# Linear attention and a soft mixture of experts on one core: three more expert weight tiles held during attention, by giving two of their slots, two input buffers and the accumulator a second use

## The chip, the cores and the metric

The kernel runs on one core of a Trainium2 chip. The metric is the device time of one execution in microseconds (us), less is better. On the core, TensorE (PE) multiplies matrices, VectorE (DVE), ScalarE (ACT) and GpSimd (POOL) do the elementwise work, and SyncE (SP) issues every DMA; each engine runs its own instructions in program order and waits on semaphores for the others.

## The reference, cut to what matters

```python
def _attn_ref(q, k, v, w_phi):            # 8 batches, 8 heads, 576 tokens, 64 columns
    def phi(x):
        proj = np.einsum('bhsd,df->bhsf', x, w_phi)
        proj = proj - np.max(np.abs(proj), axis=-1, keepdims=True)
        return np.concatenate([np.exp(proj), np.exp(-proj)], axis=-1)
    q_p, k_p = (phi(q), phi(k))
    kv = np.einsum('bhsf,bhsd->bhfd', k_p, v)
    z = np.sum(k_p, axis=2)
    num = np.einsum('bhsf,bhfd->bhsd', q_p, kv)
    den = np.einsum('bhsf,bhf->bhs', q_p, z)[..., None] + 1e-06
    return (num / den)

def _moe_ref(x, phi, w1, w2):             # x [4608, 512], 8 experts with 4 slots each, 1024 hidden
    logits = x @ phi
    d = softmax of logits over the tokens
    slot_input = d.T @ x
    slot_out[e] = max(slot_input[e] @ w1[e], 0) @ w2[e]
    c = softmax of logits over the slots
    return c @ slot_out
```

## The kernel before, in words

Heads are worked off in 32 units `u` (a pair of batches, one head, 1152 tokens, 9 tiles of 128). The keys and queries of all units lie end to end and are cut into 72 blocks `b` of 512 tokens. `proj(b)` multiplies a block of keys and the block of queries two back with `w_phi` into PSUM (`psk`, `psq`). `kmax` and `kfac` make the keys' scale factors `mk`, `kneg_exp` and `kpos_exp` the features `kf`, `vals` (POOL, L317) scales the values `vt` into `vs`, `kvmm` and `kvmid` sum `kvp` over the tokens; `num` multiplies the queries' features with it (`psn`), `scale` and `comb` join the two halves in `un`, and `denom`, `recip` and `divide` (POOL) write the attention's output into `xc` and `xn`.

These outputs are taken up in nine groups of 512 tokens. A group is turned on PE (`turn` or, for the last three, `fturn`), copied to SBUF tiles `xT`, multiplied with `moe_phi` (`logits`), and enters the running softmax over tokens (`gmax` to `update`, the accumulator is `acc`). The softmax over slots is worked on later in `call`. Then follow the experts: `layer1` (tiles `hp`, L905), `layer2` (`yp`, L979) and the outputs (`pso`, L999; copied to `o`, written to `out`).

The experts' weights are 64 tiles `wt` of 512 KB. As many as fit are loaded while attention runs (`weight`, 30 slots). Further slots lie over the buffers of attention and open when these close (`close`, `opened`), and the rest reuse the slots of the first layer's weights. `room` works the number of slots out from the sizes. Input tiles `xs` (512 KB, two blocks) have three buffers, values `vt` two.

All DMAs go through SP's one queue in program order. `load` adds two waits to it: `behind` (not before PE has passed a mark) and `deep` (not before the DMA two places earlier has landed, while attention runs).

```python
        deep = 4 if len(sent) < 9 else 2 if len(wpools) < 4 else 4 if len(wpools) < 10 else 6
```

The order of attention's work on every engine is the string `ORDER`, a letter for each step; it was made by a planner that is not part of the program. `TAIL` sets the order of layer 2 and the outputs in the same way.

Of the kernel before, what the change touches and what calls it, by code (L numbers as in the profile page):

```python
# [43 lines left out]
TRI = 3  # L44
BUFS = {'xs': 3, 'kf': 3, 'vs': 2, 'vt': 2, 'qf': 3, 'un': 2, 'xT': 4, 'xc': 2}
PICK = {'xcopy': 'adda', 'kvcopy': 'daad', 'zde': 'a'}
TOP = 212900


def room(bufs):  # L50

    parts = [XW * 4, XW * 4, XW * 4 + 2560, 4096, 4096, 4096 + bufs["vs"] * 2080 + bufs["vt"] * 2368,
             2 * 4096, 4096 + 2 * 1056, bufs["un"] * 2368, bufs["xT"] * 2048, (bufs["xc"] + 1) * G * DM * 4]
    return [int(n) // 4096 for n in np.cumsum([TOP - sum(parts)] + parts)]


class Plan:
# [42 lines left out]
ORDER = (  # L100
    "bbccbfaafhhldckiddkicgjdnoggfkglcnomhljjqbdgbdemmaprnpjjstovrrvfhfiihimmwwknvwfckndbyjjllocgehimpjqgdgfhmmprmflo"
    "jscldeihiqajmrptvwmkjbrzApnAAvvwawfsmogmejaychidpknfcgldzuhcdtlforgAjAgimknvpwrrvwohirfhjbbvwqsmykkicdnnzcgjoeml"
    "ofpjAAhitmrplrlkfqvnwvwvwjdomkmepngAcAscjtddfmolalrahryzigmfjjAvxxhkpAqrrwvvmmhknnwwyziisooceclpAAAAddgjknobgfhm"
    "tvlqrwrrjfivvwhjbwimpmmgcknstvwlknjaaocdgelxdmfyzAppAhoqrvwrvwicbbsycgrjtkdlnrffzAhodivrhibvAkwmwggnocvwfAAllhkk"
    "jjcieanyzmmoAldnojjpBpfCBhVVmmiqCbxcepddsADErftrvwgjgAmvawmhrxxFGknlopivjwmfhiBCBjHmVIcgCqdcllkjjs:eVnfDhoKqgpmr"
    "irEFkdgmLtnoJvvpxjrfhismmkHvnwcyzIwAwydzabol:tcejpfbhcKAiddaxllfhigrknAomrgAAAvwGLqvprrjmwgvxbksnowknojctefclhdm"
    "gprlfhjmxviyqdwvpfjjmmazArkwvAihnAgjjciwsepoykndctrrlxfhidlmmrovwvbggkpzfqvwjmmwkclcAJhjlAAiyempMaansfhnmptofozr"
    "hdAgvrbvirkwwbcvnrdijoAwmjmdqkggykAstneplclffocljnmoxxjhqviwdrpknozmhigdgrrvrAAAstvjaxkrfwwnjjvohwckyiNnckvwvwzA"
    "cemdAdloyzfAAnhimmpplodfBBghiVqsrVjfbbmrCCtvgjlrvAhAeapiwDvMEkOanoFmmpBGwwyVHCBVjIcgkjbd:fcchlrilCmmddgjxxnoqkPf"
    "DnoKehiExggsLmpjtrjmvvfFhblqmwprkwvnwizmaHIscjybAAepcddJ:allotfhGicKfhiAzgrmdvqwpsrxknojrrvALgAAxknkfovwwthlimNv"  # L110
    "cdycjgjllMenfgzxoprhikmmdgqvrjpjwnvoafmmwwyhcdjlAcdksAAgjfhiieznpgbmmrfbhpiarlqtvjrkoNvvwwwrAAmmysknepcAbndkjjfc"
    "zglltmvoOAhnixooAAfrmvpdrvrqwknomjmwgwhicayszdeptkvwbcfhlilgcljmApfrdjmaqnoksAAndgogvhitbrvrknrrwwycvwvwfhfhxzjj"
    "AAvwicylzxknlooemmAAppBBOdiqVgbkCVnosjcdgCfhdjPixrrmatmAlvrwvwAfvDEkhjjnwbgcFemodpmfhJHpialqBBijIgx:VmsmexCpkVCn"
    "JccoddgDtfrjbEllmhFjMgvwfrGmrknpvjwmqmhjiivHwI:aKNPxKsLkncyzoxGLfhcllyzermddAAatppqAgjrrgstokkvwnvnoAAAvmorifhcw"
    "wkvbwdcdfijexhiggncdjmplofhajyrvlmrbfmjmJgjpjhiizkAcAAwclqkvwnoyepmmddgnsgfprtlhiorMflqrvvjzhmmxivrwwAaewkyAscnt"
    "zknplfAdckbnlgoorrvoQvwAvqAhmwwjdiknrjjfmoyzmhismAAgcpepNllRSQqAtvQQARSknRrSjmvwOsTRRRwktpQQRSOryzSSyzSnrAAovwrr"
    "QUvwyyzzTAXvvRRMYwUwyzZAXRyzNSAAXXQQ4Y0Z0SS2oOTWW3W7YYZ68Q02295533665+58+5P58798+8+Q//=P<!!P=!!")

# [7 lines left out]
def tile_kernel(ctx: ExitStack, tc, xT, vv, w, phi, w1, w2, cst, out):  # L126
# [13 lines left out]
    stacks = {k: ExitStack() for k in ("x1", "x2", "x0", "k0", "k1", "v", "q1", "q2", "u", "t", "c")}  # L140

    def numbered(i, shape, name):
        return pall.tile(shape, F32, tag=f"b{i}", name=name)
# [12 lines left out]
    qp[0:2] = [pool("q1", "q1", bufs=1, side="right")] * 2  # L156
    vp = pool("v", "vp", bufs=1, side="right")
    kp = [pool(f"k{i}", f"k{i}", bufs=1, side="right") for i in (1, 0)][::-1] + [vp]
    xp = [pool(f"x{i}", f"x{i}", bufs=1, side="right") for i in (0, 2, 1)]
    xp = [xp[0], xp[2], xp[1]]  # L160

    def xtile(e):
        return xp[e % 3].tile([128, XW], F32, tag="xs", name="xs")
# [23 lines left out]
    def load(t, x, behind=False):  # L187
        i = nc.sync.dma_start(t, x).ins
        if behind and seen[2]:
            tc.add_manual_dep(i, seen[2], mybir.DependencyInfo(mybir.DependencyClass.Sync, mybir.DependencyReason.DATA), reason="behind")  # L190
        deep = 4 if len(sent) < 9 else 2 if len(wpools) < 4 else 4 if len(wpools) < 10 else 6
        if len(sent) > 3:
            tc.add_manual_dep(i, sent[-deep].name, mybir.DependencyInfo(mybir.DependencyClass.Sync, mybir.DependencyReason.DATA), reason="deep")
        sent.append(i)
# [10 lines left out]
        load(vt[u], vv[u // H, u % H], u > 1)  # L205


    call = const.tile([128, NTT, NS], F32, name="call")
    xs[1] = xtile(1)
    wx = xp[0].tile([128, 512 + FE], F32, name="wx")  # L210
    wd = wx[:, 512:512 + FE]
    load(wx, w)
    for i in 0, 512:
        load(xs[1][:, i:i + 512], xT[0][:, i:i + 512])
# [497 lines left out]
    for s in *range(NK - 4), NK - 3, NK - 2, NK - 4, NK - 1:  # L712
# [48 lines left out]
        for i, group in enumerate(groups if final else ()):  # L761
            key, pair = (m, i), (m, i // 2)

            def turn(key, group, n=n, got=got):
                ps = got[key] = bank(("turn", key), [128, 4, 128], "psx")
                for o, (kc, j) in enumerate(group):
                    nc.tensor.transpose(ps[:, o], tile4(n, j)[:, kc * 128:(kc + 1) * 128], ident)  # L767

            def keepit(key, pair, group, d, got=got, xTs=xTs):
                if (pair, "t") not in got:  # L770
                    got[pair, "t"] = xTtile(pair)
                t = got[pair, "t"][:, key[1] % 2]
# [149 lines left out]
    with tc.manual_schedule(engines={SP, PE, ACT, DVE, POOL}):  # L922
# [143 lines left out]
```

## Time and profile before

| | |
|---|---|
| median of 3 runs | 313.62 us (312.73 to 315.37) |
| the profiled execution | 316.0 us, span 314.2 us |
| PE busy | 297.1 us, 95% of the span |
| first block's products / experts' first product / last output product | 3.65 / 260.28 / 302.55 us after the span's start |

The profile is of one execution. A time in the trace is counted from the start of the span; 1.8 us of the profiled execution lie outside the span.

### The profile page before, as it was taken

How to read it: one execution, taken by the hardware profiler on the slowest of the kernel's cores; microseconds unless marked ns; L12 is line 12 of the kernel's file. 1: busy time of each engine (PE TensorE's matmuls, PEld its weight loads, DVE VectorE, ACT ScalarE, POOL GpSimd, SP SyncE). 2: the span in 40 equal slices, each digit the busy share in tenths (PEclk: the TensorE clock that was granted, in tenths of full speed). 3: DMA queues.
4: the chain of work that ended last, by engine and by line, in shares of the span. 5: the costliest groups of instructions: out<-in, count | busy, mean ns of one | idle time of the engine just before them, and what ended most of it. 6: DMA issues, size and time to landing. Idle time of an engine off the chain costs nothing.

```text
span 314.2 us, 17960 instructions
## 1 busy us (share of the span) xinstructions
PE 297.1 (95%) x7736; PEld 255.7 (81%) x7736; DVE 237.5 (76%) x706; ACT 229.4 (73%) x696; POOL 149.8 (48%) x309
## 2 busy tenths in 40 slices
PE   7999999999999799999989999999999999999970
PEld 4999999989889799998889999979998853386730
DVE  2878888968997598888968999888898867324560
ACT  4999998988878788889888889888998361003450
POOL 1657757555275566546557576446675400200000
PEclk9999999999999999999999999999999999999996
DMA  7625457667466757367666776775447999999896
GB/s 245 198 93 173 137 157 232 188 215 204 162 198 236 219 185 231 90 209 218 218 218 192 225 202 221 215 231 167 159 139 256 353 360 398 409 406 364 323 394 271
DMA packets 23119, 73.13 MB, mean 233 GB/s; under 512 B 2560, under 2 KB 2816, under 8 KB 23040
## 3 DMA queue, kind: packets, MB, share of 16 engines
q1 hardware_dynamic: 23040, 71.99, 68.5%
q8 instruction: 61, 1.00, 1.3%
q14 instruction: 18, 0.15, 0.2%
HBM read 62.54 MB, written 9.44 MB: 229 GB/s over the span
## 4 chain that ended last, share of the span: by engine, by line
PE 86%; DMA 4%; DVE 2%; ACT 2%; issue 2%; SPq 1%; POOL 0%; DVEq 0%; ACTq 0%
PE kvp L182 23%; PE psn L182 21%; PE psk L182 14%; PE psq L182 6%; PE hp L905 4%; PE yp L979 4%; PE psl L182 3%; PE psx L185 2%; DMA out<-o 2%; PE pso L999 2%; PE pss L182 2%; DMA xs<-xT 2%; PE psx L767 1%; PE psh L957 1%; DVE o L1003 1%
## 5 line engine op out<-in xcount | busy, mean ns | idle before, releaser
L317 POOL TENSOR_TENSOR vs<-vt,mk 128x520 f32<-128x520 f32 (+3 forms) x96 | 79.5, 838 | 42.7 <-DMA vt<-vv 13.4
L182 PE MATMUL kvp<-vs,kf 128*64 128x65 f32 (+1 forms) x2560 | 89.3, 223 | 2.9 <-POOL vs L317 1.8
L182 PEld LDWEIGHTS kvp<-vs,kf 128*64 128x64 f32 (+1 forms) x2560 | 82.8, 137 | 9.1 <-issue 4.8
L182 PE MATMUL psn<-kvs,qf 128*64 128x65 f32 x2304 | 78.7, 223 | 2.2 <-issue 2.1
L182 PEld LDWEIGHTS psn<-kvs,qf 128*64 128x64 f32 x2304 | 72.5, 138 | 6.7 <-issue 5.0
L182 PE MATMUL psq<-xs,wx 64*64 64x512 f32 x288 | 70.5, 601 | 1.3 <-DMA xs<-xT 0.8
L182 PE MATMUL psk<-wx,xs 64*64 64x128 f32 x1120 | 69.4, 272 | 0.0
L362 DVE TRANSPOSE_TENSOR_REDUCE mts<-psq 128x16 f32<-128x512 f32 x72 | 49.4, 701 | 13.0 <-PE psk L182 10.5
L182 PEld LDWEIGHTS psk<-wx,xs 64*64 64x64 f32 x1120 | 58.4, 133 | 0.0
L304 DVE TENSOR_REDUCE mk<-psk 128x4 f32<-128x512 f32 x72 | 47.9, 674 | 10.6 <-PE psk L182 9.6
L322 ACT ACTIVATE kf<-psk 128x512 f32<-128x512 f32 x72 | 43.0, 599 | 11.8 <-PE psk L182 8.1
L367 ACT ACTIVATE qf<-psq 128x512 f32<-128x512 f32 x72 | 42.4, 590 | 5.7 <-PE psk L182 3.2
L446 POOL TENSOR_TENSOR xc<-un,dn 128x256 f32<-128x256 f32 x62 | 37.8, 614 | 17.1 <-DVE dn L431 11.5
L325 ACT ACTIVATE kf<-psk 128x512 f32<-128x512 f32 x72 | 42.9, 600 | 0.0
L370 ACT ACTIVATE qf<-psq 128x512 f32<-128x512 f32 x72 | 42.1, 592 | 0.1
L411 DVE TENSOR_TENSOR un<-psn,eq 128x195 f32<-128x195 f32 x96 | 32.4, 345 | 7.6 <-PE psn L182 4.0
L416 DVE TENSOR_TENSOR un<-psn,un 128x195 f32<-128x195 f32 x96 | 32.0, 353 | 1.3
L378 ACT ACTIVATE mh<-mts 32x36 f32<-32x36 f32 x128 | 29.5, 230 | 3.9 <-DVE mts L362 1.6
L384 DVE TENSOR_REDUCE eq<-mh 32x9 f32<-32x36 f32 x128 | 26.1, 204 | 2.6 <-ACT mh L378 1.2
L1003 DVE COPY o<-pso 128x384 f32<-128x384 f32 x24 | 12.1, 551 | 10.3 <-PE pso L999 10.2
L182 PEld LDWEIGHTS psq<-xs,wx 64*64 64x64 f32 x288 | 15.6, 132 | 4.6 <-DMA xs<-xT 1.1
L307 ACT ACTIVATE mk<-mk 128x4 f32<-128x4 f32 x72 | 14.8, 208 | 4.5 <-DVE mk L304 3.9
(128 smaller groups left out, 307.7 us busy)
## 6 DMA issues: line engine op xcount, KB each, us to landing
wt<-w SPq DMA_DIRECT2D x64, 512.0 KB, 5.5
xs<-xT SPq DMA_DIRECT2D x35, 512.0 KB, 4.3
vt<-vv SPq DMA_DIRECT2D x32, 292.5 KB, 3.5
out<-o SPq DMA_DIRECT2D x24, 384.0 KB, 4.9
xs<-xT SPq DMA_DIRECT2D x2, 256.0 KB, 4.5
wx<-w SPq DMA_DIRECT2D x1, 320.0 KB, 2.9
cs<-cst SPq DMA_DIRECT2D x1, 128.0 KB, 2.4
phs<-phi SPq DMA_DIRECT2D x1, 64.0 KB, 3.8
```

What stands on the lines that cost most here:

```text
L182: counted(nc.tensor.matmul(*a, **k).ins, 4)
L304: nc.vector.tensor_reduce(km[b][:, 2], kx[b], axis=AX, op=ALU.max, apply_absolute_value=True)
L317: nc.gpsimd.tensor_tensor(vs[b][:, :, g + t0:g + t1], v[:, t0:t1].unsqueeze(1).broadcast_to([128, 2, n, 65]), km[b][:, 0:2, g + t0:g + t1] ...
L322: nc.scalar.activation(kf[b][:, 1], kx[b], AF.Exp, scale=-1.0)
L325: nc.scalar.activation(kf[b][:, 0], kx[b], AF.Exp)
L362: nc.vector.tensor_reduce(mts.rearrange("p r j -> p j r")[:, o:o + 4], qx[b].rearrange("p j (r t) -> p (j r) t", t=32), axis=AX, op=ALU.ma ...
L367: nc.scalar.activation(qf[b][:, 0], qx[b], AF.Exp)
L370: nc.scalar.activation(qf[b][:, 1], qx[b], AF.Exp, scale=-1.0)
L378: nc.scalar.activation(y[:, f], m[32 * f:32 * f + 32], AF.Exp, scale=-1.0)
L411: nc.vector.tensor_tensor(un[u][:, CH * c:CH * c + CH], nx[s][:, :, 0], e[:, 1].unsqueeze(2).broadcast_to([128, CH, 65]), op=ALU.mult)
L416: nc.vector.tensor_tensor(x, nx.pop(s)[:, :, 1], x, op=ALU.add)
L446: divider(u).tensor_tensor(x[:, :, h * D:(h + 1) * D], un[u][:, a:b, 0:64], dn[u][:, a:b].unsqueeze(2).broadcast_to([128, b - a, 64]), op= ...
```

## The change

The two buffers of turned tokens no longer have room of their own. Those of the first six groups lie in the last two weight slots, which get their weights when the sixth group's logits are done. Those of the last three groups lie in input buffers 0 and 2, after the last `proj`; buffers 0 and 2 move to the pool `tp` for that. The first load `wx` (first blocks and `w_phi`) lies in the last weight slot, and `w_phi` is copied from it to `wdc`. `call` holds six groups, and the last three lie over `acc`. By this 33 slots instead of 30 are there from the start, nine pools instead of eleven are closed one after the other, and 52 slots instead of 51 are there at the end. `deep` and `behind` are moved to suit the fewer closings. `ORDER` is another; `TAIL` is the same.

```diff
-TOP = 212900
+TOP = 213924
...
-    parts = [XW * 4, XW * 4, XW * 4 + 2560, 4096, 4096, 4096 + bufs["vs"] * 2080 + bufs["vt"] * 2368,
-             2 * 4096, 4096 + 2 * 1056, bufs["un"] * 2368, bufs["xT"] * 2048, (bufs["xc"] + 1) * G * DM * 4]
+    parts = [XW * 4, 4096, 4096, 4096 + bufs["vs"] * 2080 + bufs["vt"] * 2368,
+             2 * 4096, 4096 + 2 * 1056, bufs["un"] * 2368, 2 * XW * 4, (bufs["xc"] + 1) * G * DM * 4]
...
-    "bbccbfaafhhldckiddkicgjdnoggfkglcnomhljjqbdgbdemmaprnpjjstovrrvfhfiihimmwwknvwfckndbyjjllocgehimpjqgdgfhmmprmflo"
+    "bbbaacccfchfhldlfhdgiijdicmlkgjnddgkkqngonbemjpmapgdjjfohiobrrkgrsbtvvvmmnwwwyfhcdzfilojjkAAcenmlommprgphdqjmkfh"
...
-    xp = [pool(f"x{i}", f"x{i}", bufs=1, side="right") for i in (0, 2, 1)]
-    xp = [xp[0], xp[2], xp[1]]
+    xp = [tp, pool("x1", "x1", bufs=1, side="right"), tp]
...
-        deep = 4 if len(sent) < 9 else 2 if len(wpools) < 4 else 4 if len(wpools) < 10 else 6
+        deep = 4 if len(sent) < 9 else 2 if len(wpools) < 3 else 4 if len(wpools) < 8 else 6
...
-    call = const.tile([128, NTT, NS], F32, name="call")
+    call = const.tile([128, (2 * NBP - 2) * G, NS], F32, name="call")
...
-    wx = xp[0].tile([128, 512 + FE], F32, name="wx")
-    wd = wx[:, 512:512 + FE]
+    wx = wpool.tile([128, 1024], F32, tag=f"w{nslot[0] - 1}", name="wx")[:, 0:512 + FE]
+    wdc = const.tile([128, FE], F32, name="wd")
...
+    nc.vector.tensor_copy(wdc, wx[:, 512:512 + FE])
...
-        return tp.tile([128, 2, 4, 128], dt, tag=f"xT{plan.held['xT', label][0]}", name="xT")
+        i = plan.held["xT", label][0]
+        if label[0] == "z" or label[0][0] > 2 * NBP - 3:
+            return tp.tile([128, 2, 4, 128], F32, tag=f"xs{2 * i}", name="xT")
+        return wpool.tile([128, 1024], F32, tag=f"w{nslot[0] - 2 + i}", name="xT").rearrange("p (a j t) -> p a j t", a=2, j=4)
...
     def slotw(n):
+        if n > 2 * NBP - 3:
+            n -= 2 * NBP - 2
+            return acc[:, n * G * NS:(n + 1) * G * NS].rearrange("p (t s) -> p t s", s=NS)
         return call[:, n * G:(n + 1) * G]
...
-            add("fturn", key, PE, 0.056 + 0.109 * len(group), lambda t=turn, k=key, g=group: t(k, g), mode="f", lat=0.2, after=[("divide", (u, c)), ("consts", 0)],
+            add("fturn", key, PE, 0.056 + 0.109 * len(group), lambda t=turn, k=key, g=group: t(k, g), mode="f", lat=0.2, after=[("divide", (u, c)), ("consts", 0), ("proj", NB)],
...
-        add("weight", i, SP, 1.3, lambda: load_w(1), after=[("consts", 0)], at=1000)
+        add("weight", i, SP, 1.3, lambda: load_w(1), after=[("consts", 0)] + [("logits", (2 * NBP - 3, *range(KC)))] * (i > nslot[0] - 3), at=1000)
...
-    ends = [("x1", [("proj", NB - 3), ("weight", nslot[0] - 1)]), ("x2", [("proj", NB - 1)]), ("x0", [("proj", NB)]),
+    ends = [("x1", [("proj", NB - 3), ("weight", nslot[0] - 1)]),
...
-            nc.vector.transpose(ct[i][:, 0:(b - a) * 128], call[:, 4 * a:4 * b].rearrange("p t s -> p (t s)"))
+            nc.vector.transpose(ct[i][:, 0:(b - a) * 128], acc[:, 0:(b - a) * 128] if i else call.rearrange("p t s -> p (t s)"))
```

What the new `ORDER` does is shown at two places. The first is where unit 14's values are first used, in the first half of attention. On POOL, `vs` is the scaled values, made from `vt` (the second `vt` number in each piece is unit 14's tile), `dn` and `eq` are small steps of `denom` and `qsquare`, and `xc` and `xn` are `divide`. POOL before:

```order
L317 TENSOR_TENSOR vs_2556<-vt_2268,mk_2502 128x2x130
L317 TENSOR_TENSOR vs_2556<-vt_2529,mk_2502 128x2x130
L427 TENSOR_TENSOR dn_2588<-eq_2399,un_2493 128x9
L387 TENSOR_TENSOR eq_2572<-eq_2572 128x9
L388 TENSOR_SCALAR eq_2572<-eq_2572 128x9
L317 TENSOR_TENSOR vs_2696<-vt_2529,mk_2593 128x520
```

POOL after:

```order
L318 TENSOR_TENSOR vs_2604<-vt_2293,mk_2527 128x2x130
L318 TENSOR_TENSOR vs_2604<-vt_2529,mk_2527 128x2x130
L447 TENSOR_TENSOR xc_2285<-un_2328,dn_2434 128x4x64
L447 TENSOR_TENSOR xc_2059<-un_2432,dn_2570 128x4x64
L388 TENSOR_TENSOR eq_2531<-eq_2531 128x9
L389 TENSOR_SCALAR eq_2531<-eq_2531 128x9
L447 TENSOR_TENSOR xn_127<-un_2432,dn_2570 128x64
L447 TENSOR_TENSOR xc_2285<-un_2432,dn_2570 128x4x64
L318 TENSOR_TENSOR vs_2724<-vt_2529,mk_2586 128x520
```

Between the first and the second use of the tile POOL had three small steps; now it has two small ones and four of `divide`. On PE at the same place, from the second of two passes of `proj` to the first `kvp` products that need unit 14's values (in the last row of each), before:

```order
L182 MATMUL psq<-xs,wx 64x512 x2
L182 MATMUL psk<-wx,xs 64x128 x8
L182 MATMUL psn<-kvs,qf 64x65 x24
L182 MATMUL kvp<-vs,kf 64x65 x16
L182 MATMUL psn<-kvs,qf 64x65 x12
L182 MATMUL kvp<-vs,kf 64x65 x16
```

and after:

```order
L181 MATMUL psq<-xs,wd 64x512 x2
L181 MATMUL psk<-wd,xs 64x128 x8
L181 MATMUL kvp<-vs,kf 64x65 x16
L181 MATMUL psn<-kvs,qf 64x65 x24
L181 MATMUL kvp<-vs,kf 64x65 x8
L181 MATMUL psn<-kvs,qf 64x65 x24
L181 MATMUL kvp<-vs,kf 64x65 x24
```

Twelve more `psn` products now stand ahead of the products that need the tile. The second place is SP's queue from input tile 32 (the first `xs` of the piece before, the second of the two in the piece after) to input tile 34 (the last row of each); the last input tile is number 36. Before:

```order
L188 DMA xs<-xT 128x1024
L188 DMA vt<-vv 128x585
L188 DMA wt_5089<-w 128x1024
L188 DMA wt_5125<-w 128x1024
L188 DMA xs<-xT 128x1024
L188 DMA vt<-vv 128x585
L188 DMA wt_5324<-w 128x1024
L188 DMA wt_5356<-w 128x1024
L188 DMA vt<-vv 128x585
L188 DMA xs<-xT 128x1024
```

and after:

```order
L187 DMA xs<-xT 128x1024 x2
L187 DMA vt<-vv 128x585 x2
L187 DMA wt_5017<-w 128x1024
L187 DMA wt_5022<-w 128x1024
L187 DMA wt_5209<-w 128x1024
L187 DMA wt_5213<-w 128x1024
L187 DMA xs<-xT 128x1024
L187 DMA wt_5351<-w 128x1024
L187 DMA vt<-vv 128x585 x2
L187 DMA wt_5473<-w 128x1024
L187 DMA wt_5524<-w 128x1024
L187 DMA xs<-xT 128x1024
```

Eight DMAs stood between the two tiles, four of them weights; now there are twelve, seven of them weights. From tile 34 to tile 36 there were five DMAs in between and now there are three. In the whole list, the first weight stood behind 20 other DMAs and now stands behind 25; from it to the last input tile there were 82 DMAs and are 79, and one more weight follows.

## Rows read from the trace of the kernel before

**Rows 1.** The page: busy time, share of the span and instructions of each engine.

```profile
PE 297.1 (95%) x7736; PEld 255.7 (81%) x7736; DVE 237.5 (76%) x706; ACT 229.4 (73%) x696; POOL 149.8 (48%) x309
```

**Rows 2.** The page: the chain that ended last, shares of the span by engine.

```profile
PE 86%; DMA 4%; DVE 2%; ACT 2%; issue 2%; SPq 1%; POOL 0%; DVEq 0%; ACTq 0%
```

**Rows 3.** Waits of PE: line, waited for, us in total, times, longest us.

```profile
PE psn L182 <- issue: 2.1, 3, 1.0
PE kvp L182 <- POOL vs L317: 1.8, 2, 1.1
PE kvp L182 <- issue: 1.1, 2, 0.7
...
PE psq L182 <- DMA xs<-xT: 0.8, 1, 0.8
```

**Rows 4.** Timeline about unit 14's values: start, us, engine, instruction [idle before <- releaser].

```profile
101.50 0.33 SPq L188 DMA_DIRECT2D vt<-vv  x1
...
105.08 0.87 PE L182 MATMUL psn<-kvs,qf 128*64 128x65 f32 x24
...
105.93 0.62 POOL L317 TENSOR_TENSOR vs<-vt,mk 128x260 f32<-128x260 f32 x1 [3.40 <-DMA vt<-vv]
...
106.60 0.69 PE L182 MATMUL kvp<-vs,kf 128*64 128x65 f32 x16 [0.65 <-POOL vs L317]
...
107.28 1.05 POOL L317 TENSOR_TENSOR vs<-vt,mk 128x520 f32<-128x520 f32 x1
...
108.39 0.69 PE L182 MATMUL kvp<-vs,kf 128*64 128x65 f32 x16 [1.10 <-POOL vs L317]
```

**Rows 5.** The page's costliest groups, POOL's divisions: total us, mean ns of one.

```profile
L446 POOL TENSOR_TENSOR xc<-un,dn 128x256 f32<-128x256 f32 x62 | 37.8, 614 | 17.1 <-DVE dn L431 11.5
```

**Rows 6.** Timeline of SP's queue, all of the span.

```profile
57.84 0.33 SPq L188 DMA_DIRECT2D xs<-xT  x1
...
139.78 4.76 SPq L188 DMA_DIRECT2D wt<-w  x3
...
175.83 0.33 SPq L188 DMA_DIRECT2D vt<-vv  x1
...
195.58 0.33 SPq L188 DMA_DIRECT2D xs<-xT  x1
...
233.87 0.33 SPq L188 DMA_DIRECT2D xs<-xT  x1
234.27 45.99 SPq L188 DMA_DIRECT2D wt<-w  x34
```

**Rows 7.** DMA issues: KB each, median us from issue to landing.

```profile
wt<-w SPq DMA_DIRECT2D x64, 512.0 KB, 5.5
...
vt<-vv SPq DMA_DIRECT2D x32, 292.5 KB, 3.5
```

**Rows 8.** Instructions of the tile wt: ns min/median/max, first and last start; landing.

```profile
L188 SPq DMA_DIRECT2D wt<-w x64: 327/328/1665, 44.2 to 279.9; - x64
...
DMA to landing us min/median/max: 3.2/5.5/8.3
```

**Rows 9.** Busy time in 260 to 270 us, last columns PEclk, DMA share, GB/s.

```profile
260.00:270.00 10.00, 10.00 (x96) 3.28 (x99) 6.09 (x25) 1.61 (x4) 1.84 (x2) 1.00 1.02 403
```

**Rows 10.** Timeline of PE at the start and in the experts' part.

```profile
3.65 1.54 PE L182 MATMUL psk<-wx 64*64 64x128 f32 x32
...
5.03 0.59 PE L182 MATMUL psq<-xs,wx 64*64 64x512 f32 x2
...
290.57 1.95 PE L979 MATMUL yp<-wt,sh 128*32 128x128 f32 x64
...
302.55 2.94 PE L999 MATMUL pso<-ct,yt 32*128 32x384 f32 x24 [0.72 <-ACT yt L991]
```

**Rows 11.** Timeline of DVE after the accumulator's last update and in the tail.

```profile
260.79 0.29 DVE L933 STREAM_TRANSPOSE call<-part 128x128 f32<-128x128 f32 x1
...
272.18 1.43 DVE L970 STREAM_TRANSPOSE ct<-call 128x768 f32<-128x768 f32 x2
```

More of the change, by code (lines that the diff above doesn't have):

```diff
@@ L100 @@
 ORDER = (
-    "bbccbfaafhhldckiddkicgjdnoggfkglcnomhljjqbdgbdemmaprnpjjstovrrvfhfiihimmwwknvwfckndbyjjllocgehimpjqgdgfhmmprmflo"
[L102 to L115, printed above, removed]
@@ L116 @@
-    "zknplfAdckbnlgoorrvoQvwAvqAhmwwjdiknrjjfmoyzmhismAAgcpepNllRSQqAtvQQARSknRrSjmvwOsTRRRwktpQQRSOryzSSyzSnrAAovwrr"
-    "QUvwyyzzTAXvvRRMYwUwyzZAXRyzNSAAXXQQ4Y0Z0SS2oOTWW3W7YYZ68Q02295533665+58+5P58798+8+Q//=P<!!P=!!")
+    "bbbaacccfchfhldlfhdgiijdicmlkgjnddgkkqngonbemjpmapgdjjfohiobrrkgrsbtvvvmmnwwwyfhcdzfilojjkAAcenmlommprgphdqjmkfh"
+    "slctiiajjemnofplfgrhhrbavivqmvwwmwkdcliclpfcdnojrAgmhikepjmdystvggnajbdorzwfvjAAbhirplrqvwwykkmAnonofccesfhtvlgj"
+    "wmizfupdgrrjjmhikpdgvmwmhnAvwAAcalqlidkneocgpsjdtbofhjimmlrvgwrrvwvjfmmayjwqcpknosthzAAAlfceipknddgrbkjlvhmompmn"
@@ new lines @@
+    "rvwrjmwvfyzgAioqshiwjccyaakefnoAllhprknozrrdiAAqdtknbgvvfvwwwmsyxcdzcopAAdrrrthigfhjmAAgvwvwvknxjkcwyfhnilgobzAA"
+    "iemjjpllomjbBCdkpVnoBVmmAgccjCAeaddfhliDqspmExfgfhihmxtgrrrvwaxiFpkvxkwvjmjwmnoHI:BVjBVCCccyzdjnfGepllDhiKmEodqs"
+    "lAAFbgtmpbjfhgrvwkrrJvvmmwwinqLHIccstoddeyknoxa:czpjfKfllhgimGhjALgjiarrkdbnvwvwmglkorvcpqsbnoffMwAlAAheprtvyrkj"
+    "jxiNknnzdgwmhvimpwcrljfvwqkAdasgmmbhcyznoocodlAefpljihidjmrrAAmtgvqxwxkfhnoirrvvmpknsAAjmewotwpyzvwgjcaadkfhilcc"
+    "lddnjbgmmbgmjAAorpAvfhqrwrjmevxwlJxiyknckspndzffolohatvmwrvwpirAAAqrsgvwkccdgnkojjlfgtvwxxyzhilhimrAvwnorknodbfv"
@@ new lines @@
+    "wclhijAygAczAknlemompddpgaBCBVqCgjmVfhirfhjstvwbbrmrvwvAkwDEFGnjjAiemmaBBoppVCHI:MCclVqknoccdxgKdsLfDExhFjtrigmm"
+    "NxHfhvwjjGemyI:flmjpJzkOrrlnoPmviApknbvmdwwcOhxAgjydoeicdpaafhzillcKLggrAAdfhijqskmtjnorlpvvqxxMwrvwrkgfhiAnwysm"
+    "ckNcAonjjemddbtfolmhiJlggfpprjzAvahkwqrAivvwmnmkwcdjjogsyznoActbbemdMArpfAvrfamhirlkhlqpwvwmvwsjmAnxocdcknolgeir"
+    "rdyptfzbbhvkjjgnilqmmjvfhrAragAwwAsotNmvmeivpxwknywozckcpdclAAfdrnllbjhimggjvqApwrvjdfxknwfsrxtvymoozrrAAAhhiiwv"
+    "wgvknjccfakkwddgemoyzphfmphcAllxBiinjojBOVbdCqsVmngrotmCfrrDvvgkbwwnAEevwFajcklamxplxomABByhipnqdoHIjj:rCmmfPegj"
@@ L121 @@
+    "CGcVhiczpsVDdKdtvxkxEfwmngFhjJmLPgplflirjovwrvqsmhiwmbHIk:cfndxAephcyAKodlrMliaGjALftzvmhgagjkjAwqnorvwxrvAwmcpk"
+    "iAxbnosfepcfddgcyhilgmzjmtJhiflrrvwhjvrjdkAApinoammekkvOnMwwblgpcdoqjjclgnorsAlmfhrtvvyazkqijrvbnxwmpmmeAwAckwyd"
+    "ffpAzAhgoAAsinodhcrmigllqtvfjjrrvvjwwPmwymmNNpkzAhcseQtRnodgipRRrllSSSqvkkwAjmpynorvknoTRSRnoRSwUROstyrSSzzArrrA"
+    "AvwvyTwzyzvA4XYRRwyzAUvwyzAAZSSXYRXXST027Z3QWWY6QYZ09QQ802525+33Q5568868+85Q5QQ7<9W++//=!!=!!POP")
 COLS = 128
@@ L139, in tile_kernel @@
     pall = ctx.enter_context(tc.tile_pool(name="pall", bufs=1, space=PSUM))
-    stacks = {k: ExitStack() for k in ("x1", "x2", "x0", "k0", "k1", "v", "q1", "q2", "u", "t", "c")}
+    stacks = {k: ExitStack() for k in ("x1", "k0", "k1", "v", "q1", "q2", "u", "t", "c")}
     def numbered(i, shape, name):
@@ L158, in tile_kernel @@
     kp = [pool(f"k{i}", f"k{i}", bufs=1, side="right") for i in (1, 0)][::-1] + [vp]
-    xp = [pool(f"x{i}", f"x{i}", bufs=1, side="right") for i in (0, 2, 1)]
-    xp = [xp[0], xp[2], xp[1]]
+    xp = [tp, pool("x1", "x1", bufs=1, side="right"), tp]
     def xtile(e):
-        return xp[e % 3].tile([128, XW], F32, tag="xs", name="xs")
+        return xp[e % 3].tile([128, XW], F32, tag=f"xs{e % 3}", name="xs")
     xs, vt, kx, kf, km, vs, kvp, kvs = ({} for _ in range(8))
@@ L264, in load_w @@
             t = slot(i if i < nslot[-1] else order[i - nslot[-1]], f"wt{i}")
-            load(t, wsrc[i], len(wpools) < 4)
+            load(t, wsrc[i], len(wpools) < 3)
             wt.append(t)
@@ L287, in proj @@
         two = []
+        wd = wx[:, 512:512 + FE] if b == 0 else wdc
         for c in steps:
@@ L449, in tile_kernel, with xTtile @@
     ls, lTs, eTs, part = {}, {}, {}, {}
-    def xTtile(label, dt=F32):
-        return tp.tile([128, 2, 4, 128], dt, tag=f"xT{plan.held['xT', label][0]}", name="xT")
+    def xTtile(label):
+        i = plan.held["xT", label][0]
+        if label[0] == "z" or label[0][0] > 2 * NBP - 3:
+            return tp.tile([128, 2, 4, 128], F32, tag=f"xs{2 * i}", name="xT")
+        return wpool.tile([128, 1024], F32, tag=f"w{nslot[0] - 2 + i}", name="xT").rearrange("p (a j t) -> p a j t", a=2, j=4)
     def slotmm(ps, kc, t, stop=True):
```

## The prediction, made before the changed kernel ran

> **What bounds the kernel now.** The busy shares come first: PE is busy for 297.1 of 314.2 us, the next engine for 237.5 [rows 1]. The chain that ended last says the same: 86% of it is PE, 4% DMA [rows 2]. So a change counts only where PE waits, or at the end, when PE has finished. The waits of PE [rows 3] are few: 2.1 us ahead of `psn` and 1.1 us ahead of `kvp` products for nothing that the profile shows, 1.8 us for the scaled values `vs` from POOL, and 0.8 us at the start for an input. Without the start that is 5.0 us in attention, all that a better order could win from waits; beyond it only PE's own work could shrink, and its products are the same in number in both kernels.
>
> The 1.8 us are one event. SP issued unit 14's values at 101.50, behind a weight; POOL, which works in order, waited 3.40 us for them to land and began to scale them at 105.93; PE waited 0.65 us for this and 1.10 us for the next scaling, which POOL ended at 108.33 [rows 4]. So weights in SP's queue already cost PE time here, through the inputs behind them.
>
> The tail is what weights held early would help, if it waited for weights. From 260 to 270 us the DMA engines are full (403 GB/s), but PE is busy for all 10 us [rows 9], and no wait of PE for `wt` stands in its list [rows 3]. The last of the 64 weights is issued at 279.9 and, with the longest landing of 8.3 us, there by 288.2 [rows 8]. Layer 2 reads it in the last of four steps in the row at 290.57, which lasts 1.95 us [rows 10], so at about 292.0: 3.8 us to spare. Tiles land 1.3 us apart while a step of half a microsecond takes two, so the last pair is the tightest. Behind it PE sets the pace up to the last output products at 302.55 [rows 10], whose results then drain.
>
> **The change part by part.**
>
> *Fewer weights in the tail.* From 234.27 on 34 weights are left to load [rows 6]; now 31. At 403 GB/s [rows 9] a tile of 0.524 MB takes 1.30 us, so the tail's weights are there up to 3.9 us earlier. What hides this gain is PE's own work, with 3.8 us to spare for the tightest tile. I take 0. The bounds: no loss, as no load in the tail moves back; a gain of 3.9 us if loads hold PE back in a way that its rows don't show.
>
> *Three more weights in attention.* The nearest rows are the queue's own pace. From 139.78 to 175.83 SP issued 17 DMAs, 2.25 us apart [rows 6]. Each waits for the one two places earlier, and a landing takes 3.5 to 5.5 us by kind [rows 7], of which the pace is half. Over all, 82 DMAs went from the first weight at 44.2 [rows 8] to the last input at 233.87 [rows 6], 2.34 us apart. Now the first weight stands five inputs later, behind the one that was issued at 57.84, and 79 DMAs have 176.0 us: 2.23 us apart, no room left. Closest is the stretch from input tile 32, issued at 195.58, to tile 36 at 233.87 [rows 6]: 15 intervals in 38.3 us before, 17 now, which is 2.25 us apart on the dot; and 13 of the 17 lie ahead of tile 34. If inputs still come in time, as three buffers of `xs` and two of `vt` allow, this costs 0; if the queue binds, 79 x 0.02 = 1.6 us, and each value tile that comes late as unit 14's did costs 1.75 more, two of them 3.5. I take 0.4, near the low end, because in the full stretch from 139.78 no wait of PE for an input stood in its list; for the range 0 to 5.1.
>
> The Trainium skill, "DMA: Bandwidth & Descriptors", section "Anatomy of one DMA — SWDGE (gpsimd) path", gives about 2.0 us plus the bytes at 436 GB/s for one DMA by itself (fitted on GpSimd's path; here SP issues). By it a weight takes an estimated 3.2 us, two in flight go 1.6 us apart, the queue would be used to some 70% and this term would be 0. The shortest landing agrees (3.2 us [rows 8]), the median of 5.5 us [rows 7] doesn't.
>
> *The new order at unit 14's values.* PE now has 12 more `psn` products ahead of the first use. Such a product is two instructions, and 24 of those took 0.87 us with the pipeline's end [rows 4], about 0.7 us until the next could start. The wait of 0.65 us is thus covered. But POOL now has three large divisions of 0.61 us [rows 5], a small one and two small steps between the two scalings instead of three small steps: about 1.9 us more ahead of the second scaling. If the tile lands as late against PE's work as before, PE waits 1.75 - 0.7 + 1.9 = 2.95 us, a loss of 1.2 us; if it lands 3 us earlier, nothing, a gain of 1.75 us. In the new list this load stands behind eight weights in all, before it was ten, so the queue should be less behind: I take a gain of 0.8.
>
> *The new order elsewhere.* The 3.2 us of waits for nothing that shows [rows 3] are five places, two of them near 1 us. The order neither takes them away nor has a reason to add to them, but where they fall may change: 0, between -2 and +2.
>
> *What has one answer.* The copy of `w_phi` (128x128, 0.29 us as the DVE row of that size [rows 11]) can run when `wx` has landed, which is by 3.65, when PE's first products read it; the first product that reads the copy starts at 5.03 [rows 10], and DVE has no other work until then. Without that cover it would cost 0.3 us. The last groups' `fturn` stood behind the last `proj` on PE before too, so the new condition holds nothing up. The logits over `acc` are written by DVE behind its own steps that wait for PE's reading of `acc`: before, DVE begins them at 260.79 and is done at 272.18 + 1.43 [rows 11], which is hidden under the 10 us and more of the experts' first layer [rows 9]. All 0.
>
> **The sum.** 0 + 0.4 - 0.8 + 0 + 0 = -0.4 us, against the profiled execution's 316.0 us: 315.6. That execution was 2.4 us above the median of the runs shown; on the median of 313.62 the sum gives 313.2 us. This is the forecast: no change that can be told, for a measurement of this kernel tells only about 1%, 3.1 us, from none.
>
> **The rivals.**
>
> *The queue binds (slower).* Place: SP's queue between input tiles 32 and 34, near 195 to 220 us, where seven weights now stand and four stood. Mechanism: every load waits for the landing two places ahead of it, inputs fall behind, POOL and PE wait, and the buffers they free late delay the next inputs. It decides from the point at which DMAs are needed closer than 2.25 us apart, and the new list needs 2.23. Price: 1.6 us of lag and two events of 1.75, less the 0.8 won at unit 14: +4.3, 317.9 us. For it: the one wait for inputs arose behind a weight. Against: before, only one of 30 weights did this, and no wait of PE for a DMA is listed after the start.
>
> *The tail was bound by loads after all (faster).* PE's ends are modelled, so busy need not mean at work. Price: -3.9 with the sum's -0.4: 309.3 us. Against: the spare 3.8 us of the last tile.
>
> *The order is simply better (faster).* Most of the 5.0 us of waits go: -4, 309.6 us. For it: they are there to be won. Against: two thirds of them have no cause that an order removes.
>
> *The change doesn't do what it says.* Weights begin 13 us later in attention and have to catch up in a queue without room; if the last of the 33 land no earlier than the 30 did, the tail stays as it was: 313 us, inside the forecast.
>
> **How the numbers follow.** Forecast, with its own range of 310.6 to 315.8 (-0.4 with the order's 2 us and the spread of single terms): 0.63, the last rival in it. Queue 0.16, tail 0.09, better order 0.12. The range reaches to 309.5, between the two faster rivals, and to 316.9, part of the way to the slower one, which leaves out about 0.1 on either side. Faster by over 1%, below 310.5 us: the two rivals and the edge of the forecast, 0.22. Slower by over 1%, above 316.8: 0.15. Within: 0.63.
>
> **What would show it.** In the changed profile PE should wait for no `wt`, and the stretch from the experts' first product to the last output products, 42 us, should be the same within 0.5; 2 us or more shorter would mean that loads bound the tail. The last weight should be issued some 3 us earlier against the experts' first product. PE's waits for `vs` should be under 2 us in all; if they are 4 or more, or `psq` and `psk` wait for `xs` after the start, the queue binds. The prediction is wrong if the waits that have no cause in the profile move by more than 2 us, which no row here lets me foresee.

## The result, and the profile after

The changed kernel is slower: 316.67 us median against 313.81 us of the kernel before on the same chip, a ratio of 1.0113 (95% interval 1.0085 to 1.0142), some 3.5 us. The ratios leave out runs more than 1.5% above the fastest of their kernel and the medians do not: with every run the medians give 1.009 here, and 1.012 instead of 1.007 for the order alone below. Measured again on another chip the ratio was 1.014 (1.0104 to 1.0177). The forecast was 313.2 us. The profiled execution took 318.42 us with a span of 316.6.

The page first: busy time of each engine, then the chain that ended last. They stand against [rows 1] and [rows 2].

```profile
PE 298.6 (94%) x7736; PEld 255.9 (81%) x7736; DVE 239.4 (76%) x707; ACT 229.4 (72%) x696; POOL 150.1 (47%) x309
...
PE 88%; DMA 3%; DVE 2%; issue 2%; ACT 1%; POOL 1%; SPq 0%; DVEq 0%; POOLq 0%; ACTq 0%
```

PE runs the same 7736 products and still sets the end. PE's list of waits (line, waited for, us in total, times, longest), cut, stands against [rows 3]:

```profile
PE psn L181 <- issue: 2.3, 3, 1.7
PE kvp L181 <- POOL vs L318: 2.3, 2, 1.4
...
PE psq L181 <- DMA xs<-xT: 0.9, 2, 0.4
...
PE kvp L181 <- issue: 0.7, 2, 0.5
PE psx L184 <- issue: 0.6, 1, 0.6
```

The waits for `vs` did not go: they are 2.3 us after 1.8. Unit 14 is no longer among them; two other value tiles are late. The two waits for `xs` lie in the first 8 us; after the start PE waits for no input tile. The timeline about unit 12's values, in SP's queue, on POOL and on PE (start, us, instruction, in brackets the idle time before and its releaser), stands against [rows 4]:

```profile
80.51 2.74 SPq L187 DMA_DIRECT2D xs<-xT  x2
85.36 0.33 SPq L187 DMA_DIRECT2D wt<-w  x1
87.95 2.41 SPq L187 DMA_DIRECT2D vt<-vv  x2
...
91.84 1.06 POOL L318 TENSOR_TENSOR vs<-vt,mk 128x520 f32<-128x520 f32 x1 [3.47 <-ACT qf L371]
...
92.95 1.15 PE L181 MATMUL kvp<-vs,kf 128*64 128x65 f32 x32 [1.37 <-POOL vs L318]
```

SP issued the values at 87.95, behind two inputs and a weight; by the trace they land 3.74 us later, at 91.69, and POOL starts at 91.84. (The releaser ACT in brackets is one that the profile names; the tile that POOL reads is `vt`.) The same once more at unit 28, with five weights ahead:

```profile
199.38 8.07 SPq L187 DMA_DIRECT2D wt<-w  x4
208.79 0.33 SPq L187 DMA_DIRECT2D xs<-xT  x1
211.43 0.33 SPq L187 DMA_DIRECT2D wt<-w  x1
213.42 3.11 SPq L187 DMA_DIRECT2D vt<-vv  x2
...
218.41 2.07 POOL L318 TENSOR_TENSOR vs<-vt,mk 128x520 f32<-128x520 f32 x2 [2.47 <-PE psn L181]
...
219.52 1.15 PE L181 MATMUL kvp<-vs,kf 128*64 128x65 f32 x32 [0.95 <-POOL vs L318]
```

The four weights were issued (8.07 - 0.33) / 3 = 2.58 us apart, slower than the 2.25 us of the forecast, so the input tile behind them went out at 208.79 and the values only at 213.42. Unit 28's values then took 4.85 us to land, 1.4 us above their median, so in this execution a slow landing has a share in PE's 0.95 us. In the second profile of this kernel they took 3.94 us, and of PE's waits

```profile
PE kvp L181 <- POOL vs L318: 1.6, 2, 1.3
```

1.30 us are at unit 28 and 0.31 at unit 12. The median landings are near what they were [rows 7] (KB, median us):

```profile
wt<-w SPq DMA_DIRECT2D x64, 512.0 KB, 5.2
xs<-xT SPq DMA_DIRECT2D x35, 512.0 KB, 4.4
vt<-vv SPq DMA_DIRECT2D x32, 292.5 KB, 3.5
```

The 64 weights include those of the tail. The 32 that were issued in attention have a median of 4.4 us; in the kernel before the 30 in attention had 4.6.

The tail is unchanged. The experts' first product starts at 262.6, and the last output products at

```profile
304.99 1.57 PE L1006 MATMUL pso<-ct,yt 32*128 32x384 f32 x16 [0.72 <-ACT yt L998]
```

so the stretch takes 42.4 us; before it was 302.55 [rows 10] less 260.3, 42.3. In these two profiles the loss lies in attention.

### The profile page after: what moved, and what is told of

It is laid out like the page before. It is cut to its first block, busy times and chain, and to the rows that moved or that the text cites. A ratio compares the mean times of both kernels' runs of the same rounds, so it can differ in the third digit from the quotient of the medians.

```text
span 316.6 us, 17982 instructions
## 1 busy us (share of the span) xinstructions
PE 298.6 (94%) x7736; PEld 255.9 (81%) x7736; DVE 239.4 (76%) x707; ACT 229.4 (72%) x696; POOL 150.1 (47%) x309
## 4 chain that ended last, share of the span: by engine, by line
PE 88%; DMA 3%; DVE 2%; issue 2%; ACT 1%; POOL 1%; SPq 0%; DVEq 0%; POOLq 0%; ACTq 0%
PE kvp L181 23%; PE psn L181 22%; PE psk L181 14%; PE psq L181 6%; PE yp L986 4%; PE hp L912 4%; PE psl L181 3%; PE pso L1006 3%; PE psx L184 2%; PE pss L181 2%; DMA xs<-xT 2%; PE psx L774 1%; DMA out<-o 1%; PE psh L964 1%; DVE o L1010 1%
## 5 line engine op out<-in xcount | busy, mean ns | idle before, releaser
L181 PE MATMUL psn<-kvs,qf 128*64 128x65 f32 x2304 | 77.6, 223 | 3.0 <-issue 2.3
L181 PE MATMUL psq<-xs,wd 64*64 64x512 f32 x288 | 70.5, 600 | 0.9 <-DMA xs<-xT 0.9
L181 PE MATMUL psk<-wd,xs 64*64 64x128 f32 x1120 | 69.8, 272 | 0.0
L181 PEld LDWEIGHTS psk<-wd,xs 64*64 64x64 f32 x1120 | 58.8, 133 | 0.3 <-issue 0.3
L323 ACT ACTIVATE kf<-psk 128x512 f32<-128x512 f32 x72 | 42.9, 599 | 18.1 <-PE psk L181 12.4
L388 POOL TENSOR_TENSOR eq<-eq 128x9 f32<-128x9 f32 x32 | 6.6, 205 | 27.0 <-DVE eq L385 26.9
L181 PEld LDWEIGHTS psq<-xs,wd 64*64 64x64 f32 x288 | 15.7, 132 | 3.3 <-DMA xs<-xT 0.7
```

The costliest lines, as they stand in the source:

```text
L181: counted(nc.tensor.matmul(*a, **k).ins, 4)
L323: nc.scalar.activation(kf[b][:, 1], kx[b], AF.Exp, scale=-1.0)
```

## The experiments

Each ratio is against the kernel before, measured beside it on the same chip, with its 95% interval. In the short edits w, V and X are a weight, a value tile and an input tile in SP's list, by number, and Q is a closing.

**The layout alone.** The old order in the new layout:

```diff
- (SP, order of before)  V31 X36 Q Q Q Q ...
+                        V31 X36 w30 w31 w32 Q Q ...
```

> The order of before with the layout of after: 33 weight slots, turned tokens in late slots and input buffers, logits over the accumulator; two of the three closings fall away and the three extra weights stand behind the last input load. Against before (1.000). If the weights ahead of inputs cost the time: no extra weight stands ahead of an input, so 0.997 to 1.003. If the new order of PE's work costs it: the same, 0.997 to 1.003. If the layout itself costs it (buffers shared with the turned tokens, the copy of w_phi, the logits behind the accumulator): 1.008 to 1.014, as the changed kernel.

Measured: 1.0008 (0.9982 to 1.0035). The layout, with the copy of `w_phi`, the shared buffers and the logits over `acc`, costs nothing that can be told.

**The order alone.**

```diff
- (SP, order of after)  X31 X32 V26 V27 w25 w26 w27 w28 X33 w29 V28 V29
+ (layout of before)    X31 X32 V26 V27 w25 w26 X33 V28 V29
```

> The layout of before (30 weight slots, own buffers for the turned tokens) with the order of after, less the three weights numbered 27 to 29 of its list, which stand ahead of inputs. Against before. If the three extra weights in SP's queue cost the time: 0.996 to 1.003, and POOL's wait for unit 28's values is gone. If the new order costs it by itself: 1.008 to 1.014, and PE's waits for nothing that the profile shows stay above those of before by 2 us or more. If the layout costs it: 0.997 to 1.003.

Measured: 1.007 (1.0034 to 1.0107), between the two theories. In the profiled execution unit 28's wait is gone and unit 12's was 0.2 us; with 312.5 us it is one of the four fastest of twelve, so it doesn't show what the others lost.

**Three weights behind the inputs.** The same three letters, in the new layout, moved behind X36.

> The changed kernel with one edit: weights 27 to 29 of its list stand behind the last input load instead of ahead of the last values. Against before, where the changed kernel has 1.011. If the queue costs the time at its most crowded stretch: the wait of PE for unit 28's scaled values (2.1 us with the weight load's) goes, 1.002 to 1.006. If the order of PE's work costs it: 1.009 to 1.014, no different from the changed kernel.

Measured: 1.004 (1.0008 to 1.0071). This kernel and the one of the order alone have the same list up to the last input; against the changed kernel's 1.011 to 1.014 the three weights are worth 0.4 to 1.0%, 1 to 3 us. Unit 28's wait is gone here too; PE still waits 1.2 us for `vs`, half of it at unit 12.

**Three loads in flight.** The changed kernel, one number:

```diff
-        deep = 4 if len(sent) < 9 else 2 if len(wpools) < 3 else 4 if len(wpools) < 8 else 6
+        deep = 4 if len(sent) < 9 else 3 if len(wpools) < 3 else 4 if len(wpools) < 8 else 6
```

> The changed kernel with three loads of SP in flight during attention instead of two. Against before. If SP's queue of two, each load behind the landing two places ahead, is what makes the values late: both late events (units 12 and 28, 3 to 4 us of PE's time) go, 0.998 to 1.003, and gaps between SP's issues shrink below 2.25 us where it has work. If the order costs it: 1.009 to 1.014. If landings grow as more are in flight (the bandwidth is what binds), no gain either: the landing of a weight goes from a median of 5.5 to about 8 us.

Measured: 0.9984 (0.9954 to 1.0014). The loss is gone. PE's waits in full:

```profile
PE psw L218 <- POOL call L214: 0.9, 1, 0.9
PE pso L1006 <- ACT yt L998: 0.7, 1, 0.7
PE psq L181 <- DVE mk L305: 0.7, 1, 0.7
PE kvp L181 <- issue: 0.5, 1, 0.5
PE psn L181 <- DVE xT L801: 0.3, 1, 0.3
PE psk L181 <- DMA wx<-w: 0.3, 1, 0.3
```

No wait for `vs` is left. The timeline of SP's queue at unit 28:

```profile
194.45 6.78 SPq L187 DMA_DIRECT2D wt<-w  x4
202.97 0.33 SPq L187 DMA_DIRECT2D xs<-xT  x1
203.35 0.42 SPq L187 DMA_DIRECT2D wt<-w  x1
207.12 1.81 SPq L187 DMA_DIRECT2D vt<-vv  x2
```

The four weights are (6.78 - 0.33) / 3 = 2.15 us apart, and the values go out 12.67 us after the first of them, where it was 14.04 us. The third load in flight did stretch these weights: three of the four took 6.43, 6.24 and 5.43 us to land, where they had taken 4.95, 5.24 and 4.34, so the pace gained a sixth and not a third. But the median landings of inputs and values, for which PE waits, are within 0.1 us of the changed kernel's: the wait for the landing two places ahead bound here more than the bandwidth.

**The changed kernel again**, for the next three.

> The changed kernel once more, unedited, on the chip of the three kernels that follow, so that their ratios stand beside its own. Against before: 1.0085 to 1.0142 again if the loss is the kernel's; nearer to 1.000 if it was the chip's of the first measurement.

Measured: 1.014 (1.0104 to 1.0177).

**The kernel before with three in flight** (2 to 3 in the same line of before).

> The kernel before with three loads of SP in flight during attention instead of two. If the queue of two binds before as well: unit 14's late values (1.8 us) go and nothing else, 0.993 to 0.997. If the depth helps by something other than late values, it helps here as much as it did in the changed kernel (about 1.3%): 0.985 to 0.990. If before is not held up by the queue beyond what jitter does: 0.998 to 1.002.

Measured: 0.9948 (0.992 to 0.9975). PE's wait for `vs` falls from 1.8 us to

```profile
PE kvp L182 <- POOL vs L317: 0.3, 1, 0.3
```

and that one is at 10 us: unit 14's is gone. The ratio is worth 1.6 us. So two loads in flight instead of three cost 1.6 us before and (1.014 - 0.9984) x 311.4 = 4.9 us after (the two ratios are from two chips); the change added 3.2, give or take 1.7 by the three intervals.

That is what the depth is worth, and late values are only a part of it. Each kernel can be set beside its run with three in flight product by product, since PE runs the same products in the same order. The changed kernel comes out 7.3 and 5.1 us longer in its two profiles: 3.1 and 2.3 us arise about units 12 and 28, and 4.1 and 1.4 us at waits without a cause. The kernel before is 5.6 us longer in its profile, 2.1 of it about unit 14 and 3.2 at such waits. In these single executions late values thus grew by 0.2 to 1.0 us; the rest of the 3.2 us isn't found in them.

**Four weights moved, all 33 held, two in flight.**

```diff
- X14 X15 w6 V12 V13 X16      ...  w25 w26 w27 w28 X33 w29 V28 V29 w30 w31 X34
+ X14 X15 V12 V13 w6 X16      ...  w25 w26 X33 V28 V29 w27 w28 w29 w30 w31 X34
```

> The changed kernel with two loads in flight as it has them, all 33 weights in attention, and four of them moved by a few places in SP's list: weight 6 from ahead of unit 12's values to behind unit 13's, weights 27 to 29 from ahead of unit 28's values to behind unit 29's. Against before. If the loss is the weights just ahead of two value tiles: PE's waits for vs fall from 2.3 us to under 0.5, 0.999 to 1.004. If it is the count of 79 loads in a queue without room, the lag moves to the next inputs (unit 30's values, input tile 34) and PE waits there: 1.006 to 1.012. If it is the order of PE's own work: 1.009 to 1.014.

Measured: 1.0228 (1.0177 to 1.0278), worse than any expectation. The waits for `vs` are gone as meant, and input tile 34, now behind five weights, is late instead. The timeline of SP's queue and of PE:

```profile
213.72 8.75 SPq L187 DMA_DIRECT2D wt<-w  x5
224.35 0.33 SPq L187 DMA_DIRECT2D xs<-xT  x1
...
228.89 1.11 PE L181 MATMUL psq<-xs,wd 64*64 64x512 f32 x2 [4.07 <-DMA xs<-xT]
```

And the windows before, just after and later (length; busy time and instructions of PE, PEld, DVE, ACT, POOL; granted clock, DMA share, GB/s):

```profile
220.00:228.80 8.80, 4.76 (x155) 4.44 (x152) 5.71 (x16) 6.42 (x21) 4.47 (x9) 0.99 0.77 249
228.80:232.40 3.60, 3.51 (x44) 3.37 (x46) 1.37 (x3) 0.58 (x3) 1.20 (x2) 0.56 0.58 190
232.40:242.00 9.60, 9.60 (x311) 9.36 (x312) 8.40 (x29) 8.12 (x25) 7.65 (x17) 1.00 0.38 132
```

PE waits 4.07 us in one piece. The granted clock is then 0.56, nearly the lower of its two levels, for 3.6 us, in which PE does what would take an estimated 2 us (0.56 x 3.6). The lag in the queue was not a matter of one place: it was handed on to the input behind the next weights.

**Weights begun earlier, all 33 held, two in flight.** Weights 6 and 26 to 28 leave their places; four go to 45 to 57 us:

```diff
- X9 V7 X10 V8 V9 X11 w0 w1 X12 X13        ...  X15 w6 V12  ...  V27 w25 w26 w27 w28 X33
+ X9 V7 w w X10 w V8 w V9 X11 w w X12 X13  ...  X15 V12     ...  V27 w X33
```

> The changed kernel with two loads in flight and all 33 weights in attention, four of them moved forward in SP's list: weights 6, 26, 27 and 28 leave the places just ahead of late inputs, and four weights go to 44 to 55 us, where SP waits for buffers and not for its queue. Against before. If the loss is the queue without room: 0.996 to 1.003, PE's waits for vs under 0.5 us. If only the last stretch is relieved and unit 12's values stay late: 1.003 to 1.006. If it is the order of PE's work: 1.006 to 1.012.

Measured: 1.0137 (1.0089 to 1.0185): nothing won. Units 12 and 28 are in time, and the late tile is now the input behind the early weights. SP's queue and PE:

```profile
54.01 0.33 SPq L187 DMA_DIRECT2D vt<-vv  x1
56.51 0.33 SPq L187 DMA_DIRECT2D wt<-w  x1
57.31 1.13 SPq L187 DMA_DIRECT2D vt<-vv  x1
60.25 0.33 SPq L187 DMA_DIRECT2D xs<-xT  x1
...
65.28 0.65 PE L181 MATMUL psq<-xs,wd 64*64 64x512 f32 x2 [1.92 <-DMA xs<-xT]
```

My expectation was wrong in taking 44 to 55 us as free; the changed kernel's SP waited for buffers there, but with room for fewer loads than four: input tile 11 went out at 60.25 instead of 56.84. By the ratio alone this run can't tell the queue from the order; the next can.

**The new order with 30 weights and three in flight.**

> The layout of before with the order of after less three weights, as in the run that gave 1.007, and three loads in flight. Against before. If its 0.7% was the queue: 0.994 to 0.999. If it was the order of the engines' work: 1.004 to 1.008.

Measured: 1.0009 (0.9979 to 1.0039), after 1.007 with two. So most of what the order alone cost came with the depth of two, and a rest stays: against the old order with three in flight (0.9948, interval to 0.9975) it is 0.6%, 1.9 us, and in the new layout (0.9984 against 0.9931 below) 0.5%, 1.7 us.

**The best of both**: old order, new layout, three in flight; and four in flight with either order.

> The new layout with the old order (the three extra weights behind the last input) and three loads in flight: the candidate for a kernel better than both. Against before. If nothing but unit 14's late values is left to win: 0.993 to 0.997. If the tail is bound by loads and the three extra weights help it: 0.985 or less, with the stretch from the experts' first product to the last output products below 41 us. If the queue's lateness is covered anyway with this order: 0.998 to 1.002.

Measured: 0.9931 (0.9906 to 0.9956), 309.26 us against 311.4: faster than both kernels, and no different from the old layout with three in flight (0.9948).

> The changed kernel with four loads of SP in flight in attention. Against before. With three it is at 0.998, the old order in the same layout at 0.993. If the 0.5% between them is still the queue: 0.993 to 0.996. If it is the new order of the engines' work: 0.997 to 1.000, as with three. If four in flight stretch the landings of what is needed first: above 1.000.

Measured: 1.0018 (0.9989 to 1.0047), not to be told from three in flight (0.9984).

> The old order in the new layout with four loads in flight. Against before; with three it is at 0.993. If three already free the queue: 0.991 to 0.996, the same. If more depth still helps: below 0.990. If the landings stretch: above 0.996.

Measured: 1.0007 (0.998 to 1.0035). Four in flight is no better than three with either order, and with the old one worse. The expectations have stretched landings for that, but the medians of inputs and values are within 0.2 us of those with three; the profile lists no late input, and 1.2 us of its waits are ones without a cause, so why is open.

**What held weights are worth in the tail.** The kernel before with the last three, or six, of its 30 weights left to the tail, each run once:

> The kernel before with 27 weights held in attention instead of 30: the last three weights of its list are loaded when the first input buffer is given up, with the rest. If the tail is PE's own and its tightest weight has some 3.8 us to spare: the stretch from the experts' first product to the last output products stays at 42.3 us, within 0.5. If loads bind the tail, each weight at 1.30 us: 46.2 us.

Measured: the stretch from the experts' first product (254.1) to the last output products is 43.9 us, and of it 1.0 us are two waits without a cause that the kernel before hasn't:

```profile
283.58 0.86 PE L979 MATMUL yp<-wt,sh 128*32 128x128 f32 x23 [0.58 <-issue]
...
295.58 0.38 PE L979 MATMUL yp<-wt,sh 128*32 128x128 f32 x2 [0.38 <-issue]
...
297.96 2.94 PE L999 MATMUL pso<-ct,yt 32*128 32x384 f32 x24 [0.72 <-ACT yt L991]
```

So 42.9 without them, 0.6 above 42.3; no wait for `wt` is listed. (The first of the two stands at the same product as one of 0.9 us in the layout alone, which has more weights held.)

> The kernel before with 24 weights held in attention instead of 30. If some 3.8 us are to spare: six weights at 1.30 us are 7.8 us, of which 4.0 show: the stretch from the experts' first product to the last output products goes from 42.3 to about 46.3 us. If loads bind the tail already: 50.1 us. If much more is to spare than the last weight's landing shows: 42.3 us still.

Measured: 256.2 to 309.70, 53.5 us, 11.2 more, and more than any of the expectations. PE's wait for weights in its list:

```profile
PE yp L979 <- DMA wt<-w: 5.3, 8, 0.9
```

Two of its eight places in the timeline:

```profile
291.63 0.43 PE L979 MATMUL yp<-wt,sh 128*32 128x128 f32 x8 [0.84 <-DMA wt<-w]
292.91 0.65 PE L979 MATMUL yp<-wt,sh 128*32 128x128 f32 x8 [0.85 <-DMA wt<-w]
```

The windows there and behind:

```profile
286.20:296.20 10.00, 5.31 (x87) 2.14 (x86) 1.09 (x3) 0.86 (x2) 0.00 (x0) 0.83 1.02 408
296.20:306.20 10.00, 9.53 (x136) 5.58 (x138) 3.36 (x7) 2.75 (x7) 0.00 (x0) 0.66 1.01 401
```

With six fewer PE follows the loads, one tile each 1.28 us (291.63 to 292.91) at 408 GB/s; then the granted clock falls, and the same eight products take 0.65 instead of 0.43 us.

## Why the prediction was wrong

**The step that failed** is the term "Three more weights in attention", taken at 0.4 us, "near the low end, because in the full stretch from 139.78 no wait of PE for an input stood in its list". It was mis-sized: the runs with two and three in flight give some 3.2 us (2.4 with the first measurement), and the runs with the three weights behind the inputs put these at 1 to 3 us. The queue was judged by its average pace, 2.25 us, against an average need of 2.23; but the two are the same queue: where it has work its pace is about half of what landings take at that moment, 2.58 us at unit 28's weights, which landed in 4.3 to 5.2 us, and a stretch that showed no wait only showed that the old order's uses lay far enough behind. That the old list already made PE wait 1.8 us at unit 14 was in [rows 4], and I read it as one event to be won and not as the sign of a queue at its limit. The Trainium skill, "DMA: Bandwidth & Descriptors", section "Anatomy of one DMA — SWDGE (gpsimd) path", gives by the estimate in the prediction a queue used to some 70%; the traces don't agree: in attention a weight landed in 4.4 us (median), not 3.2. The prediction's own 5.5 us for a weight was the median of all 64 and too long for the 30 in attention, which had 4.6.

**The rival that came true** is "The queue binds": every load waits for the landing two places ahead, and one more in flight takes the loss away. It said +4.3 us, measured were +3.5 and +4.4. That this is so near is in part luck: its price has nothing for the order, and by the profiles two late events account for less of it than it says. Nor did its sign show: the prediction asked for 4 us or more of waits for `vs` or a wait for `xs` after the start, and there were 2.3 and 1.6 us and none. It took the runs with three in flight to see it. Its place was half right, since one of the two late tiles was unit 28's, behind five of the seven weights it names, and the other unit 12's. The argument against it, that only one of 30 weights did this before, counted events in one execution. The bounds did hold the term (0 to 5.1), but the range stopped at 316.9, and +3.5 on the median of 313.62 is 317.1.

**Unit 14's values**: the gain came, the wait is gone; but with the same order unit 12 is late by 1.37 us in the first profile and 0.31 in the second, so of the -0.8 little or nothing was left.

**The order elsewhere**, taken at 0 (±2): with three in flight the new order still costs 0.5 to 0.6%, 1.7 to 1.9 us, inside the bounds. The listed waits of the two orders with three in flight hardly differ; PE's busy time on the pages is 297.0 and 297.3 us with the new order and 296.3 and 296.0 with the old. So some 1 us lies in how the same products run one behind the other, which the prediction took as equal; why is not settled.

**The waits without a cause**, 3.2 us before, from which the rival of a better order drew its 4 us: in attention they are 3.7 us in the changed kernel's first profile and 1.4 in its second, and 0 to 1.8 in the other kernels. With the old order they were 3.2 us before and 0 with the layout alone, so they come and go without a change of order, and counting on an order to win them had no ground.

**Right**: the tail. Its stretch stayed at 42.4 us against 42.3, so the tail was not bound by loads. The spare time of 3.8 us was about right for three weights and no guide for six, where a clock that falls comes on top. The last weight was issued 1.2 us earlier against the experts' first product (281.1 less 262.6, before 279.9 less 260.3) and not some 3 us. That is not the last rival's lag: the last input went out 30.0 us ahead of the experts' first product, before 26.4. Behind it SP waited for other engines, that is for slots to open, 18.1 us where it had been 6.6 (234 to 282 us), most of it in

```profile
SPq L187 <- PE kvp L181: 5.8, 3, 4.1
SPq L187 <- PE psn L181: 4.1, 1, 4.1
```

Right too: the terms with one answer, as the layout alone shows (1.0008).

In sum: depth of two +3.2, order and layout together +1.1 (0.9984 against 0.9948). By the way they are taken these make up the second measurement, 0.014 x 311.4 = +4.4 us, so they divide it and don't check it; the first was +3.5.

## What to carry to other kernels

A load queue that holds each load behind a landing two places ahead goes at the pace of the landings of the moment: if one tile is late behind a prefetch already, more prefetch in it can cost what the average pace doesn't show, and in both tries moving the prefetches by hand only changed which tile was late. Before adding loads, try one more in flight: here that was worth more than the three slots, for the kernel before as well, and a fourth won nothing. Then look at how much of the gain stands in the waits that it was to remove; here it was under half. And ask first whether the stretch that the prefetch should help waits for it at all; here three weights fewer changed the tail by some 0.6 us in one run, and three more by nothing.

## What the runs showed of the hardware that was not expected

After one wait of PE of 4.07 us the granted clock was 0.56 for the next 3.6 us, near the lower of its two levels (1.2 of 2.4 GHz), and 1.00 after that; after one of 1.92 us it stayed at 1.00 (PE's two `psq` products took 0.65 us there, 1.11 us behind the longer wait). In a row of seven waits of 0.57 to 0.86 us it fell too, to 0.83 and 0.66 over two stretches of 10 us. The Trainium skill, "TensorE: Matmul & The Clock Gate", section "HAM oscillation — how this bites in real kernels", has the products after a wait for loads start at the slow clock: the wait of 4.07 us agrees, the one of 1.92 us doesn't. So a late load can cost more than its wait.

The waits without a cause stand at the same few instructions of PE's program in different runs: product 4401 of 7736 (counted from 0) in four runs of the new order with two in flight (0.23 to 1.1 us) and in none of its runs with three or four in flight, product 5034 in two (1.66 and 1.44 us), product 4405 in two runs of the old order (0.98 and 0.70); but product 348 in the changed kernel (0.17 us) and in its runs with three (0.54) and four (1.20) in flight. The profile names no releaser. It does list a DMA queue of instructions (transfers, MB, share of 16 engines):

```profile
q8 instruction: 61, 1.00, 1.3%
```

These are 61 transfers of 16 KB. All 34 waits without a cause in the 16 profiles end 1.05 to 1.54 us after the end of one of them, a place that by chance a tenth of them would have. And the products at which they stand are multiples of 126.75 products apart (within 0.03 of a whole one), as 7736 products in 61 pieces would be (126.8). So PE most likely waits there for the next piece of its own program; a releaser that says so is not on record. Whether SP's loads make these pieces late is open: the waits sum to 0.2 to 3.7 us in the ten profiles with two loads in flight, and to 0 to 1.2 us in the six with three or four.
